# Early weight conversions subtract on VectorE instead of GpSimd, and ScalarE copies out all transposes of the first five head pairs

## The chip, the cores and the metric

The kernel runs on one core of one Trainium2 chip. Five engines work side by side: TensorE multiplies matrices (PE in the profile, and PEld where it loads weights), VectorE (DVE) and ScalarE (ACT) work on rows of 128 partitions and can read the accumulators in PSUM, GpSimd (POOL) works on SBUF alone here, and SyncE (SP) issues the DMA transfers. Each engine runs its own instructions strictly in order, and an instruction that waits for another engine holds up everything behind it. The metric is the device time of one execution in microseconds (us); less is better.

## The reference

Two stages. The first is attention over 4 batches of 8 heads, 576 rows of 64, with a memory term mixed in by a gate per head; the second is a feed-forward block over the 2304 rows of the result.

```python
scores = scale * np.matmul(q, k.transpose(0, 1, 3, 2))     # causal, then softmax: a
local = np.matmul(a, v)
q_p = phi(q)                                               # phi(x) = (x if x > 0 else exp(x) - 1) + 1
mem_out = einsum(q_p, M_prev) / (einsum(q_p, z_prev)[..., None] + 1e-06)
attn = g * mem_out + (1 - g) * local                       # g = sigmoid(beta), one per head
x = attn.transpose(0, 2, 1, 3).reshape(B * S, H * D)       # 2304 x 512
h = x @ w_in                                               # 512 -> 2048
y = (h * np.tanh(log1p(exp(h)))) @ w_out                   # 2048 -> 512, float32
```

The weights `w_in` and `w_out` come as 64-bit floats, and the products of the second stage are made from a high and a low part of each operand.

## The kernel before

**Attention** goes by pairs of heads, 16 in all. For a pair `load`, `load2` and `loadv` bring the inputs; `scores` multiplies (line 364, tile `s`), takes the scores out of PSUM with the running row extreme (line 374, VectorE, tiles `w` and `mx`) and makes the exponentials in place (line 381, ScalarE); `prep` makes phi(q) and its denominators (lines 313 to 337, tiles `qn`, `phe`, `den`; the product with `z` is GpSimd's). `norm` scales the exponentials by the row sums and puts phi(q) beside them (lines 93 and 87 as GpSimd's, tile `w`). `transp` then transposes the weights of one head on TensorE (line 445, tile `t` in PSUM) in four groups of 384, 448, 512 and 512 columns, and each group is copied to SBUF (tile `at`): by ScalarE at line 110 or by VectorE at line 112. These copies are called evictions here. `av` multiplies with the values (line 473, tile `vps`), ScalarE makes the high part `xo` and VectorE the low part `xl`, and both go to memory (`xs`).

**Conversion of weights.** `split` makes one of 16 slices of both weight matrices ready, in two calls of `narrow`, one for `wi` and one for `wo`. Such a half is a DMA into `raw` and seven steps: `c1` scales the upper word on ScalarE (line 91, tile `wa`) and takes its sign on VectorE (line 156, tile `ws`); `c2` is lines 162 and 165 on VectorE; `c3` makes the high part `hi` on ScalarE (line 110); `c4` is line 172 on VectorE, the last reader of `raw`; `c5` subtracts `hi` from `wa` (line 178, recorded at its helper, line 87); `c6` adds the rest on VectorE (line 87 again) and frees `wa` and `ws`. Six slices, twelve halves, are converted between the pairs 1 to 6 (`CV`), with one buffer each for `raw`, `wa` and `ws`; ten more follow after the attention, with a subtraction of their own name (`wsut`). The table `ENG` names the engine of each step: `wsub` is the subtraction of the first twelve halves.

**Feed-forward.** From pair 4 on, pieces of its first part are mixed in (`steps_a`): 12 products for a block of 128 hidden columns (line 233, tile `h`), Mish on ScalarE (line 217, which needs another function table than the exponential, so that ScalarE loads tables between them), a high part on ScalarE and a low part on VectorE (tile `g`), and after six blocks the products with `w_out` (line 246). After the last pair `tail` does the rest (lines 566 and 583).

**What sets the order.** The code is recorded in program order with priorities (`OFF`), and a scheduler lays out each engine's instructions from a simulated run; at run time that order is fixed. A change of an engine at one step can therefore move other instructions, on every engine. The functions that the diff touches:

Of the kernel before, what the change touches and what calls it, by code (L numbers as in the profile page):

```python
# [30 lines left out]
VB = 2  # L31
CV = {1: 1, 3: 1, 4: 2, 5: 1, 6: 1}
FAE = "avav"
CB = 1
CT = 2
RT = 2
# [4 lines left out]
GPB = 6  # L41
NRM = "ppppp"
ENG = {"ph2": "v", "mghT": "a", "mglT": "v", "min": "v", "zmul": "p", "cphi": "p", "xlo": "v",
       "mgh": "a", "mgl": "v", "wx": "a", "whi": "a", "wsub": "p", "wadd": "v", "wsut": "v", "wadt": "v"}
QT = [(0, 64), (64, 192), (192, 320), (320, 448), (448, 576)]
BIG = 8.0e9
E_SC = 0.125
# [29 lines left out]
def attention_moe_kernel(ctx: ExitStack, tc: tile.TileContext, f_src, qn, vn, zz, beta, w_in, w_out, out):  # L77
# [30 lines left out]
    def copy(which, o, i):  # L108
        if which == "a":
            nc.scalar.copy(out=o, in_=i)  # L110
        elif which == "v":
            nc.vector.tensor_copy(out=o, in_=i)  # L112
        else:
            nc.gpsimd.tensor_scalar(out=o, in0=i, scalar1=1.0, scalar2=1.0, op0=ALU.mult, op1=ALU.mult)
# [30 lines left out]
    def narrow(pool, own, src, hi, lo):  # L145
        t = {}

        def c0():
            t["r"] = raw = pool.tile([128, 512, 2], I32, tag="raw", name="raw", bufs=1 if own is cp else RT)
            t["a"] = own.tile([128, 512], I32, tag="e", name="wa", bufs=CB if own is cp else CT)  # L150
            t["s"] = own.tile([128, 512], I32, tag="L", name="ws", bufs=CB if own is cp else CT)
            nc.sync.dma_start(out=raw[:].rearrange("p a b -> p (a b)"), in_=src.bitcast(I32))
# [111 lines left out]
    def attention():  # L264
# [17 lines left out]
        def spare(p, order, pool, tag, shape):  # L282
            if p < EARLY and order[turn[tag] % len(order)] == "e":
                pool = ps_e
            turn[tag] += 1
            return pool.tile(shape, F32, tag=tag, name=tag)
# [145 lines left out]
        def transp(h):  # L432
            g = hd[h]
            ops = []

            def tr(gr, first):
                if first:
                    g["at"] = []
                g["at"].append(tp.tile([128, 512], F32, tag="at", name="at", bufs=AHB))
                ps = g["tps"] = spare(h // 2, TQ, ps_t, "t", [128, 512])  # L440
                o = 0
                for t, m in gr:
                    n = QT[m][1] - QT[m][0]
                    c = WO[m] + 128 * t
                    nc.tensor.transpose(ps[:, o:o + 128], g["w"][:, c:c + 128], ident[:])  # L445
                    o += n

            def out(base, n):
                copy(FAE[base], g["at"][base][:, :n], g["tps"][:, :n])

            for base, gr in enumerate(GR):
                n = sum(QT[m][1] - QT[m][0] for _, m in gr)
                ops += [lambda gr=gr, first=(base == 0): tr(gr, first), lambda base=base, n=n: out(base, n)]
            return ops
# [52 lines left out]
        for p in range(NP):  # L507
# [16 lines left out]
            if p >= P0:  # L524
                if (p - P0) % 4 == 0:
                    todo.extend(steps_a((p - P0) // 4))
                n = int(SPREAD * (p - P0 + 1)) - done[0]
# [142 lines left out]
```

## Time and profile before

| what | us |
|---|---|
| runs shown | 656.19, 655.2, 653.29; median 655.2 |
| the profiled execution, its own time | 654.77 |
| its span, first to last instruction | 653.0 |
| busy: PE, PEld, DVE, ACT, POOL | 597.0, 454.9, 336.8, 300.7, 169.1 |

The page's picture in 40 slices of 16.3 us; each digit is the busy share in tenths:

```profile
PE   3477968889989999999998979999999999999997
PEld 2254635656655766767776878888888888888886
DVE  4989897765588654573338887920311211121121
ACT  3677655866567675566325455621222222222221
POOL 3697886464166714443000000000000000000000
PEclk9979986899999999999999989999999999999999
```

TensorE is busy nearly throughout, but a busy PE is not a PE at its peak, since matmuls wait in it; its gaps lie in the first ten slices, where VectorE has its highest digits. GpSimd ends its work with the attention, at slice 20.

### The profile page before, as it was taken

How to read it: one execution, taken by the hardware profiler on the slowest of the kernel's cores; microseconds unless marked ns; L12 is line 12 of the kernel's file. 1: busy time of each engine (PE TensorE's matmuls, PEld its weight loads, DVE VectorE, ACT ScalarE, POOL GpSimd, SP SyncE). 2: the span in 40 equal slices, each digit the busy share in tenths (PEclk: the TensorE clock that was granted, in tenths of full speed). 3: DMA queues.
4: the chain of work that ended last, by engine and by line, in shares of the span. 5: the costliest groups of instructions: out<-in, count | busy, mean ns of one | idle time of the engine just before them, and what ended most of it. 6: DMA issues, size and time to landing. Idle time of an engine off the chain costs nothing.

```text
span 653.0 us, 9308 instructions
## 1 busy us (share of the span) xinstructions
PE 597.0 (91%) x3200; PEld 454.9 (70%) x3200; DVE 336.8 (52%) x903; ACT 300.7 (46%) x694; POOL 169.1 (26%) x260
## 2 busy tenths in 40 slices
PE   3477968889989999999998979999999999999997
PEld 2254635656655766767776878888888888888886
DVE  4989897765588654573338887920311211121121
ACT  3677655866567675566325455621222222222221
POOL 3697886464166714443000000000000000000000
PEclk9979986899999999999999989999999999999999
DMA  6345674324275226421257765304302220430220
GB/s 229 104 144 182 189 262 150 133 61 144 76 235 168 98 62 176 166 73 58 91 176 235 261 206 176 121 1 129 130 0 82 94 83 6 124 129 0 65 97 33
DMA packets 47007, 80.83 MB, mean 124 GB/s; under 512 B 7280, under 2 KB 21616, under 8 KB 46960
## 3 DMA queue, kind: packets, MB, share of 16 engines
q1 hardware_dynamic: 46960, 80.24, 38.0%
q8 instruction: 25, 0.41, 0.3%
q14 instruction: 22, 0.18, 0.1%
HBM read 61.35 MB, written 18.87 MB: 123 GB/s over the span
## 4 chain that ended last, share of the span: by engine, by line
PE 61%; DVE 13%; DMA 10%; ACT 7%; POOL 5%; issue 2%; SPq 1%; DVEq 0%; ACTq 0%; POOLq 0%
PE o L583 19%; PE h L566 19%; PE acc L246 7%; PE h L233 5%; DMA raw<-in_w_in_dram 5%; PE vps L473 5%; PE t L445 4%; DVE w L374 3%; PE s L364 3%; POOL w L93 3%; DMA raw<-in_w_out_dram 3%; DMA qn<-in_qn_dram 2%; ACT w L381 2%; ACT L217 1%; DVE ws L172 1%
## 5 line engine op out<-in xcount | busy, mean ns | idle before, releaser
L87 DVE TENSOR_TENSOR g<-u,g 128x512 fp32r<-128x512 f32 (+1 forms) x80 | 52.4, 661 | 185.6 <-ACT g L110 185.6
L566 PE MATMUL h<-xb,wi 128*128 128x512 f32 (+1 forms) x600 | 134.9, 368 | 0.0
L583 PE MATMUL o<-wo,g 128*128 128x512 f32 x540 | 133.8, 390 | 0.0
L217 ACT ACTIVATE u<-h 128x512 f32<-128x512 f32 (+1 forms) x80 | 43.5, 554 | 179.2 <-PE h L566 170.9
L566 PEld LDWEIGHTS h<-xb,wi 128*128 128x128 f32 x600 | 106.1, 188 | 19.6
L583 PEld LDWEIGHTS o<-wo,g 128*128 128x128 f32 x540 | 100.6, 188 | 20.3
L93 POOL TENSOR_SCALAR w<-w,rc 128x64 f32<-128x64 f32 (+4 forms) x160 | 95.4, 621 | 71.0 <-ACT w L381 53.3
L381 ACT ACTIVATE w<-w,mx 128x576 f32<-128x576 f32 (+4 forms) x160 | 88.3, 554 | 28.5 <-DVE mx L374 27.6
L364 PE MATMUL s<-f 64*128 64x288 f32 (+4 forms) x384 | 69.2, 472 | 31.7 <-DVE mx L374 25.4
L233 PE MATMUL h<-xb,wi 128*128 128x512 f32 (+1 forms) x360 | 88.0, 389 | 7.8 <-ACT u L217 7.8
L246 PE MATMUL acc<-wo,g 128*128 128x512 f32 x324 | 85.9, 401 | 1.4 <-ACT ob L110 0.9
L445 PE MATMUL t<-ident,w 128*128 128x128 f32 x480 | 75.5, 291 | 5.3 <-ACT at L110 3.1
L233 PEld LDWEIGHTS h<-xb,wi 128*128 128x128 f32 x360 | 64.8, 200 | 21.1 <-ACT u L217 9.6
L364 PEld LDWEIGHTS s<-f 64*128 64x128 f32 x384 | 35.4, 207 | 59.0 <-DVE mx L374 33.2
L445 PEld LDWEIGHTS t<-ident,w 128*128 128x128 f32 x480 | 55.9, 146 | 26.0 <-issue 8.7
L246 PEld LDWEIGHTS acc<-wo,g 128*128 128x128 f32 x324 | 59.4, 190 | 16.0 <-issue 2.3
L374 DVE CUSTOM_DVE_ANT_0 w<-s,mask 128x288 f32<-128x288 f32 (+4 forms) x160 | 59.6, 421 | 17.6 <-PE s L364 17.6
L473 PE MATMUL vps<-at,v 128*64 128x256 f32 (+2 forms) x512 | 61.3, 383 | 5.8 <-DVE xl L87 3.7
L473 PEld LDWEIGHTS vps<-at,v 128*64 128x64 f32 x512 | 35.6, 142 | 31.7 <-issue 6.0
L112 DVE COPY at<-t 128x448 f32<-128x448 f32 x64 | 41.5, 649 | 16.2 <-PE t L445 16.2
L110 ACT CAST g<-u 128x512 fp32r<-128x512 f32 (+1 forms) x80 | 45.5, 579 | 1.8
L110 ACT COPY at<-t 128x384 f32<-128x384 f32 x64 | 33.7, 526 | 17.6 <-PE t L445 17.4
(45 smaller groups left out, 432.1 us busy)
## 6 DMA issues: line engine op xcount, KB each, us to landing
f<-in_f_src_dram SPq DMA_DIRECT2D x32, 288.0 KB, 3.7
raw<-in_w_in_dram SPq DMA_DIRECT2D x16, 512.0 KB, 3.9
raw<-in_w_out_dram SPq DMA_DIRECT2D x16, 512.0 KB, 3.5
xb<-xs SPq DMA_DIRECT2D x24, 256.0 KB, 3.7
qn<-in_qn_dram SPq DMA_DIRECT2D x16, 320.0 KB, 3.4
v<-in_vn_dram SPq DMA_DIRECT2D x16, 320.0 KB, 3.3
xs<-xo SPq DMA_DIRECT2D x16, 288.0 KB, 3.4
xs<-xl SPq DMA_DIRECT2D x16, 288.0 KB, 3.3
```

What stands on the lines that cost most here:

```text
L87: engines[ENG[name]].tensor_tensor(**kw)
L93: engines[which].tensor_scalar(out=o, in0=i, scalar1=scale, scalar2=1.0, op0=ALU.mult, op1=ALU.mult)
L110: nc.scalar.copy(out=o, in_=i)
L233: ins = nc.tensor.matmul(ps, wi[y, f][:, c, :], x[c][:, z], start=(q == 0), stop=(q == 11))
L246: nc.tensor.matmul(acc[:], g[:, y, 128 * t:128 * t + 128], wo[z, f], start=(f == 0 and y == z), stop=(f == KA - 1 and z == 1),)
L364: nc.tensor.matmul(g["ps"][:, o:o + n], f[le, 0, q0:q0 + 128], f[le, 1, a:b], start=True, stop=True)
L374: nc.vector.tensor_tensor_reduce(out=g["w"][:, WO[m] + D + a:WO[m] + D + b], in0=g["ps"][:, o:o + n], in1=mask[:, c0:c0 + n], scale=-E_SC, ...
L381: nc.scalar.activation(out=row, in_=row, func=ACTF.Exp, scale=-1.0, bias=g["mx"][:, m:m + 1], accum_out=g["sm"][:, m:m + 1])
L445: nc.tensor.transpose(ps[:, o:o + 128], g["w"][:, c:c + 128], ident[:])
L473: queued(nc.tensor.matmul(ps[64 * e:64 * e + 64, a:b], d["v"][:, t, e], at[e][gi][:, c:c + b - a], start=(k == 0), stop=(k == last),), k o ...
L566: nc.tensor.matmul(ps[:, :n], wi[a, f][:, c, :], x[c][:, b], start=(k == 0), stop=(k == 11))
L583: nc.tensor.matmul(D_[t][:], g[:, y, 128 * t:128 * t + 128], wo[z, f], start=(f == KA and y == z), stop=(f == NF - 1 and z == 1),)
```

## The change

Two edits and a constant. `wsub` goes from GpSimd (`"p"`) to VectorE (`"v"`): the subtraction `c5` of the twelve early halves. And with `EVA = 5` the evictions of the pairs 0 to 4 (heads 0 to 9) are all ScalarE's; before, the groups 1 and 3 of every head were VectorE's. Later heads keep the alternation `"avav"`.

```diff
 FAE = "avav"
+EVA = 5
 ...
 ENG = {...
-       ..., "wsub": "p", "wadd": "v", "wsut": "v", "wadt": "v"}
+       ..., "wsub": "v", "wadd": "v", "wsut": "v", "wadt": "v"}
 ...
             def out(base, n):
-                copy(FAE[base], g["at"][base][:, :n], g["tps"][:, :n])
+                copy("a" if h // 2 < EVA else FAE[base], g["at"][base][:, :n], g["tps"][:, :n])
```

The new line moves every later line number of the kernel by one: line 112 of before is 113 after, and so on. Counted over the whole program, 20 copies `at<-t` leave VectorE for ScalarE (ten of 448 columns and ten of 512), 12 subtractions `wa<-wa,wi` and `wa<-wa,wo` leave GpSimd for VectorE, and ScalarE loads its tables 20 times instead of 18.

The order also moves. First VectorE, from the reduction of `den` of the fourth pair on. `wi_2`, `wo_1` are halves of slices 2 and 1, high part first. Before:

```order
L332 TENSOR_REDUCE den<-phe 128x10
L87 TENSOR_TENSOR xl<-vps,xo 128x320
L112 COPY at<-t 128x448
L374 ISA w,mx<-s,mask 128x288
L374 ISA mx 128x1
L87 TENSOR_TENSOR wo_1_85<-wa,ws 128x512
L417 TENSOR_SCALAR rc<-sm,gt 128x5
L333 SCALAR_TENSOR_TENSOR den<-den,gt 128x10
L313 TENSOR_SCALAR phe<-qn 128x640
L374 ISA w,mx<-s,mask 128x288
L374 ISA mx 128x1
L112 COPY at<-t 128x512
```

After, the same place:

```order
L333 TENSOR_REDUCE den<-phe 128x10
L88 TENSOR_TENSOR xl<-vps,xo 128x320
L88 TENSOR_TENSOR wa<-wa,wi_2_86 128x512
L375 ISA w,mx<-s,mask 128x288
L375 ISA mx 128x1
L375 ISA w,mx<-s,mask 128x288
L375 ISA mx 128x1
L334 SCALAR_TENSOR_TENSOR den<-den,gt 128x10
L314 TENSOR_SCALAR phe<-qn 128x640
L418 TENSOR_SCALAR rc<-sm,gt 128x5
L88 TENSOR_TENSOR wi_2_88<-wa,ws 128x512
```

The two copies are gone, a subtraction has come, and the conversion stands one half further: where `wo_1` ended, `wi_2` ends now.

Next ScalarE around the same place, from the high part `xo` of the first pair's output on. Before:

```order
L110 CAST xo<-vps 128x320
L110 COPY at<-t 128x384
L381 ACTIVATE w,sm<-w,mx 128x320
L381 ACTIVATE w,sm<-w,mx 128x192
L381 ACTIVATE w,sm<-w,mx 128x320
L381 ACTIVATE w,sm<-w,mx 128x192
L110 COPY at<-t 128x512
L91 ACTIVATE wa<-raw 128x512
```

After:

```order
L111 CAST xo<-vps 128x320
L111 COPY at<-t 128x384
L111 CAST wi_2_86<-wa 128x512
L111 COPY at<-t 128x448
L382 ACTIVATE w,sm<-w,mx 128x320
L382 ACTIVATE w,sm<-w,mx 128x192
L382 ACTIVATE w,sm<-w,mx 128x320
L382 ACTIVATE w,sm<-w,mx 128x192
L111 COPY at<-t 128x512 x2
L111 COPY at<-t 128x384
```

Two more evictions stand among the exponentials, and the cast that makes `wi_2`'s high part stands behind an eviction.

Last ScalarE where the feed-forward begins, from the first table load for Mish on. Before:

```order
L217 ACT_TABLE_LOAD
L217 ACTIVATE u<-h 128x512
L381 ACT_TABLE_LOAD
L381 ACTIVATE w,sm<-w,mx 128x448
L381 ACTIVATE w,sm<-w,mx 128x64
L110 CAST g<-u 128x512
L91 ACTIVATE wa<-raw 128x512
L217 ACT_TABLE_LOAD
L217 ACTIVATE u<-h 128x512
L110 COPY at<-t 128x512
L110 CAST g<-u 128x512
L110 CAST wi_5_98<-wa 128x512
```

After:

```order
L218 ACT_TABLE_LOAD
L218 ACTIVATE u<-h 128x512
L382 ACT_TABLE_LOAD
L382 ACTIVATE w,sm<-w,mx 128x576
L92 ACTIVATE wa<-raw 128x512
L111 COPY at<-t 128x384
L111 CAST g<-u 128x512
L218 ACT_TABLE_LOAD
L218 ACTIVATE u<-h 128x512
L111 CAST wo_5_99<-wa 128x512
L111 CAST g<-u 128x512
L111 COPY at<-t 128x512
```

The conversion is again one half further: `wi_5`'s cast, in this stretch before, is done ahead of it now, and what is left is the last half, `wo_5`.

## Rows read from the trace of the kernel before

**Rows 1.** Busy time by stretch: us, engines with instruction counts, PEclk, DMA share, GB/s.
```profile
40.00:60.00 20.00, 18.48 (x133) 12.49 (x133) 19.32 (x65) 14.99 (x44) 15.70 (x23) 0.91 0.44 142
60.00:80.00 20.00, 17.73 (x129) 11.57 (x125) 18.14 (x52) 12.13 (x35) 17.66 (x24) 0.91 0.64 201
80.00:100.00 20.00, 12.53 (x79) 7.37 (x78) 18.59 (x53) 11.73 (x32) 15.46 (x20) 0.89 0.76 247
100.00:120.00 20.00, 18.26 (x98) 12.00 (x98) 16.43 (x49) 10.46 (x26) 14.82 (x18) 0.77 0.46 147
120.00:140.00 20.00, 17.40 (x79) 12.00 (x78) 12.99 (x35) 18.05 (x33) 9.72 (x15) 0.91 0.18 62
140.00:160.00 20.00, 16.77 (x107) 11.89 (x104) 11.86 (x38) 13.05 (x32) 6.92 (x12) 1.00 0.50 155
...
260.00:280.00 20.00, 20.00 (x126) 14.19 (x127) 11.29 (x40) 11.85 (x36) 9.15 (x17) 1.00 0.44 148
```

**Rows 2.** Chain that ended last, 20 to 160 us: start, us, what.
```profile
40.29 0.60 DVE at L112
...
88.00 3.46 DMA raw<-in_w_out_dram
...
98.81 0.60 DVE at L112
...
109.64 4.03 DMA raw<-in_w_out_dram
...
123.92 0.57 ACT wa L91
...
127.39 0.52 ACT wi L110
```

**Rows 3.** Groups by form, whole span: line, engine, op, count | busy us, mean ns | idle before.
```profile
L172 DVE SCALAR_TENSOR_TENSOR ws<-raw,ws 128x512 f32<-128x512 uint32 x32 | 24.6, 768 | 0.5
L112 DVE COPY at<-t 128x512 f32<-128x512 f32 x32 | 21.8, 682 | 7.5 <-PE t L445 7.5
L112 DVE COPY at<-t 128x448 f32<-128x448 f32 x32 | 19.7, 615 | 8.7 <-PE t L445 8.7
L110 ACT COPY at<-t 128x512 f32<-128x512 f32 x32 | 18.5, 579 | 8.0 <-PE t L445 7.9
...
L217 ACT ACT_TABLE_LOAD x9 | 11.5, 1283 | 2.7 <-PE h L233 2.6
...
L87 POOL TENSOR_TENSOR wa<-wa,wo 128x512 f32<-128x512 f32 x6 | 8.0, 1340 | 0.0
...
L87 DVE TENSOR_TENSOR wa<-wa,wo 128x512 f32<-128x512 f32 x10 | 6.8, 685 | 0.0
```

**Rows 4.** Groups by form on VectorE, 20 to 105 us alone.
```profile
L172 DVE SCALAR_TENSOR_TENSOR ws<-raw,ws 128x512 f32<-128x512 uint32 x7 | 7.2, 1028 | 0.1
...
L332 DVE TENSOR_REDUCE den<-phe 128x10 f32<-128x640 f32 x7 | 5.7, 814 | 4.2 <-POOL phe L87 4.2
L162 DVE SCALAR_TENSOR_TENSOR wa<-wa,ws 128x512 int32<-128x512 int32 x7 | 5.5, 785 | 0.0
...
L313 DVE TENSOR_SCALAR phe<-qn 128x640 f32<-128x640 f32 x6 | 4.0, 671 | 0.0
```

**Rows 5.** Instructions in order of time, 64 to 69 us: start, us, engine, what [idle before].
```profile
64.63 1.65 DVE L313 TENSOR_SCALAR phe<-qn 128x640 f32<-128x640 f32 x1
64.65 1.27 POOL L87 TENSOR_TENSOR wa<-wa,wi 128x512 f32<-128x512 f32 x1
...
67.65 1.62 POOL L93 TENSOR_SCALAR w<-w,rc 128x64 f32<-128x64 f32 x2 [1.73 <-DVE den L337]
```

**Rows 6.** Waits, 20 to 160 us: who for whom, us in total, times, longest.
```profile
POOL wa L87 <- ACT wi L110: 8.0, 1, 8.0
...
PE t L445 <- ACT at L110: 2.5, 3, 1.1
...
PE vps L473 <- DVE at L112: 1.8, 2, 1.3
```

More of the change, by code (lines that the diff above doesn't have):

```diff
@@ L43 @@
 ENG = {"ph2": "v", "mghT": "a", "mglT": "v", "min": "v", "zmul": "p", "cphi": "p", "xlo": "v",
-       "mgh": "a", "mgl": "v", "wx": "a", "whi": "a", "wsub": "p", "wadd": "v", "wsut": "v", "wadt": "v"}
+       "mgh": "a", "mgl": "v", "wx": "a", "whi": "a", "wsub": "v", "wadd": "v", "wsut": "v", "wadt": "v"}
 QT = [(0, 64), (64, 192), (192, 320), (320, 448), (448, 576)]
```

## The prediction, written before the changed kernel ran

> **What bounds the kernel now.** I read the busy time by stretch first, since the change touches only the first 150 us. From about 160 us on TensorE is full: in the stretch 260 to 280 us it is busy 20.00 of 20 and ScalarE and VectorE are not [rows 1]. The order of all engines from the last pair's attention on is the same in both kernels. So the change can move the end only by what it does before 160 us, and what is won there passes to the end in full. How much there is to win: TensorE's gaps are 3.8 us in 40 to 80 us (40 less 18.48 and 17.73) and 15.0 us in 80 to 160 us (80 less 12.53, 18.26, 17.40 and 16.77) [rows 1]. That 18.8 us is the ceiling for these stretches.
>
> What fills the gaps' place is VectorE: 19.32, 18.14 and 18.59 of 20 in the three stretches from 40 to 100 us. GpSimd is high too (15.70, 17.66, 15.46), ScalarE is not (14.99, 12.13, 11.73). After that the load turns round: in 120 to 140 us ScalarE is busy 18.05, VectorE 12.99, GpSimd 9.72 [rows 1].
>
> Second, the chain of waits. Between 20 and 105 us it runs for the most part through VectorE, and ten of its pieces there are evictions of VectorE, from 40.29 to 98.81 us, 0.60 us each at most, some 5 us. Pieces of the early conversion are on it as well: two loads of `raw` (3.46 and 4.03 us), and in ScalarE's stretch a scaling of 0.57 and a cast of 0.52 us [rows 2]. The subtraction on GpSimd does not appear on it.
>
> **The subtraction leaves GpSimd.** Twelve at 1.34 us is 16.1 us less on GpSimd [rows 3]. I count this as worth nothing by itself: the subtractions stand in GpSimd's gaps. At 64.65 us one runs for 1.27 us, and GpSimd then still idles 1.73 us until VectorE's `den` lets it scale the next head [rows 5]. What it does to VectorE is another matter: in the same moment the simple operation at line 313 takes 1.65 us, where the other five of its group in 20 to 105 us take (4.0 - 1.65)/5 = 0.47 us [rows 4, 5]. One such stretch of 1.2 us goes with the subtraction.
>
> **The subtraction comes to VectorE.** No subtraction of the early halves has run there. The late ones, when GpSimd is idle, take 0.685 us [rows 3]; that is the lower end, 8.2 us for twelve. The upper end is line 172, also 512 columns with two inputs, in the stretch where GpSimd is busy: 1.028 us, against (24.6 - 7.2)/25 = 0.70 us in the other 25 cases [rows 3, 4]; twelve of these are 12.3 us. I take line 162 in that stretch, the nearest in form (two inputs of the same width, `wa` among them): 0.785 us, 9.4 us in all.
>
> The trace thus shows VectorE's two-input operations lengthened while GpSimd works. The Trainium skill, GPSIMD Engine Reference, section Specifications, says why: GpSimd's SBUF interfaces are shared with VectorE, with contention for VectorE's operations in a two-port mode or with two SBUF inputs. The rule speaks against moving a two-input operation to VectorE while GpSimd still has its scalings to do; by it the sum would lie toward 12.3 us, and by line 162's row it is 9.4.
>
> **The evictions.** Ten copies of 448 columns at 0.615 us and ten of 512 at 0.682 us leave VectorE: 13.0 us [rows 3]. ScalarE gets ten of 512 at 0.579 us and ten of 448 that it has not done before, at most 0.579 us each and surely above half of that: 8.7 to 11.6 us, I take 11. They lie in 20 to 118 us, where ScalarE has a quarter to two fifths of its time free (8.3 us of 20 in 80 to 100 us, 5.0 in 40 to 60 us) [rows 1]; I cost them there at nothing. If that cover fails, the price shows at TensorE's transposes, which wait for a free PSUM tile: they waited 2.5 us for ScalarE's evictions in 20 to 160 us, and twice the evictions would make it 5.0. Against that, the 1.8 us that the products with the values waited for VectorE's evictions go [rows 6]. The net, +0.7 us, I put into the sum.
>
> VectorE's balance is therefore -13.0 + 9.4 = -3.6 us (bounds -4.8 and -0.7). The order shows when it arrives: counting instructions up to the last scores of the sixth pair, the new order has 18 copies fewer but nine subtractions more and two halves of conversion further on, and the load is the same; only by the eighth pair, when both orders have converted all twelve halves, is the difference there. Since VectorE is the fullest engine until 100 us and the conversions that are done earlier are missing from the later stretch, I take the 3.6 us in full.
>
> **What moves on ScalarE.** In 120 to 140 us ScalarE is the full engine. The order shows one scaling and one cast of a conversion fewer there, both on the chain: 0.57 + 0.52 = -1.1 us [rows 2]. Two more table loads, 1.283 us each [rows 3], come later, where TensorE is full and ScalarE has 8 us of 20 free [rows 1]: zero, at worst +2.6.
>
> **The sum.** -1.2 (stretch) -3.6 (VectorE) -1.1 (ScalarE) +0.7 (waits for evictions) = -5.2 us, from the profiled execution's own 654.77 us: 649.6. That execution is 0.4 us below the median of the three runs, so against the median it is 650.0, 0.8% less. It is under a third of the 18.8 us of gaps. The ends: with the dear subtraction, the stretch and the 1.1 us not gained and the tables paid, -0.7 + 0.7 + 2.6 gives 658; with the cheap one and VectorE's 4.2 us of waiting for GpSimd's `phe` [rows 4] filled by conversion work pulled forward, about 645.
>
> **Rivals.**
> *Nothing moves.* TensorE in 40 to 80 us has only 3.8 us of gaps, so relief of VectorE there ends in TensorE, and after 105 us the chain goes over table loads, scalings of GpSimd and transfers that the change leaves alone. For it: VectorE's load up to the sixth pair is unchanged by the order. Against it: 15 us of gaps lie in 80 to 160 us. Time 655.
>
> *Slower: VectorE stands still at the new subtraction.* It needs the cast that ScalarE makes of the same half. On GpSimd such a wait harmed nobody: one lasted 8.0 us [rows 6]. On VectorE it holds back all behind it: the scores of the next pair, then ScalarE's exponentials, then TensorE. And the order puts a cast behind evictions now (`wi_2` behind the copy of 384 columns), which wait for transposes, which wait for GpSimd's scalings. Against it: in most places of the new order there is a score step or more between line 172 and the subtraction. One stall like that of GpSimd gives 650.0 + 8.0 = 658, two give 666; from 5.2 us of stalls in all it is no gain.
>
> *A larger gain.* The early halves are a chain of their own, since each waits for the one buffer `raw`; two loads of it, 3.46 and 4.03 us, are on the chain of waits [rows 2]. With the conversion two halves ahead these would fall where VectorE has other work: 650.0 - 7.5 = 642.5. Against it: VectorE itself idled little at these places, its neighbours were as late.
>
> **How the numbers follow.** A measurement of this kernel can tell a difference of about 0.5%, 3.3 us: faster is under 651.9, slower over 658.5. The forecast, -5.2 us, has a chance of 0.43, and its own range is 646 to 654. Nothing moves: 0.27. Slower: 0.20. Larger gain: 0.10. Of the forecast some 0.34 lie under 651.9, with the larger gain 0.44 faster; same gets 0.38, with the rest of the forecast and the lighter end of the stalls; slower 0.18. The range is 643 to 661: it leaves out two long stalls above and a gain beyond both terms below.
>
> **What would show it.** Right: VectorE under 18.5 of 20 in the stretches from 40 to 100 us or the eighth pair's scores done earlier; the subtractions at 0.69 to 1.03 us; no wait of VectorE's `wa` for ScalarE's `wi` or `wo` in the list of waits beyond 2 us; the last attention product and the first late load of `raw` some 5 us earlier and the rest unchanged. Wrong: that wait at 5 us or more; TensorE's transposes waiting over 5 us for ScalarE's evictions; a 120 to 160 us stretch in which ScalarE is as full as before.

## The result, and the profile after

The changed kernel takes 661.62 us (median of 8 runs, 659.23 to 663.74) against 655.91 us of the kernel before on the same chip: a ratio of 1.0085, interval 1.0063 to 1.0107. It is 0.85% slower, where 650.0 us was forecast. The profiled execution took 662.05 us, its span 660.0 us.

Busy time by stretch of the kernel after, with the columns of [rows 1]; two stretches are new here:

```profile
40.00:60.00 20.00, 16.89 (x114) 10.90 (x116) 18.65 (x64) 16.29 (x44) 13.75 (x19) 0.83 0.41 137
60.00:80.00 20.00, 17.29 (x126) 10.98 (x123) 16.01 (x47) 13.89 (x38) 19.95 (x28) 0.91 0.69 219
80.00:100.00 20.00, 13.32 (x87) 8.11 (x87) 18.73 (x53) 13.89 (x37) 11.50 (x15) 0.91 0.70 225
100.00:120.00 20.00, 16.11 (x88) 10.45 (x88) 16.22 (x49) 13.29 (x35) 14.67 (x19) 0.83 0.58 188
120.00:140.00 20.00, 18.96 (x105) 13.89 (x104) 12.36 (x39) 18.07 (x37) 2.49 (x5) 1.00 0.21 65
140.00:160.00 20.00, 19.02 (x114) 14.09 (x114) 10.80 (x35) 12.81 (x30) 5.81 (x11) 1.00 0.37 114
180.00:200.00 20.00, 14.61 (x103) 8.88 (x102) 11.92 (x46) 10.71 (x32) 10.78 (x21) 0.93 0.57 177
260.00:280.00 20.00, 18.59 (x99) 13.69 (x100) 12.05 (x39) 11.69 (x34) 7.20 (x11) 0.91 0.37 116
```

The stretch 180 to 200 us of the kernel before, which the prediction did not look at:

```profile
180.00:200.00 20.00, 17.75 (x134) 11.43 (x133) 15.92 (x54) 12.62 (x36) 14.49 (x28) 1.00 0.67 210
```

VectorE is relieved from 60 to 80 us (16.01 for 18.14), and GpSimd fills there instead (19.95 for 17.66). TensorE gains from 120 to 160 us (18.96 and 19.02 for 17.40 and 16.77) what it lost before. Then, far behind the last moved instruction, it is busy 3.1 us less from 180 to 200 us and 1.4 us less from 260 to 280, both at a granted clock under 1.00.

Chain that ended last, 20 to 160 us, of the kernel after (start, us, what), some of its longest pieces:

```profile
47.28 3.81 POOL w L94 x5
...
72.33 4.03 POOL w L94 x4
...
86.24 1.84 DVE wa L88
93.24 3.04 DMA qn<-in_qn_dram
...
147.12 1.28 ACT L319
```

Where [rows 2] has evictions of VectorE and loads of `raw`, there is now one new subtraction on VectorE (1.84 us) and a table load at line 319, and most of the long pieces are scalings of GpSimd. Those were on the chain before too, but with less: line 93 was 10.1% of it between 20 and 105 us, line 94 is 32.5%. That subtraction in order of time:

```profile
85.99 1.54 POOL L88 TENSOR_TENSOR phe<-qn,z 128x640 f32<-128x640 f32 x1 [0.76 <-DVE qn L85]
86.17 1.92 DVE L88 TENSOR_TENSOR wa<-wa,wo 128x512 f32<-128x512 f32 x1
```

Waits of the kernel after, 20 to 160 us, as in [rows 6]:

```profile
POOL w L94 <- DVE rc L421: 18.5, 1, 18.5
...
DVE den L333 <- POOL phe L88: 9.0, 6, 2.7
...
PE t L446 <- ACT at L111: 7.2, 6, 2.2
...
PE vps L474 <- ACT at L111: 1.5, 2, 1.2
...
DVE wa L88 <- ACT wo L111: 0.9, 1, 0.9
```

Where a pair's second store into `xs` is issued tells roughly how far the whole program is (us, one traced execution of each kernel; e1 to e10 are the experiments below):

| pair | before | after | e1 | e2 | e4 | e5 | e6 | e7 | e9 | e10 |
|---|---|---|---|---|---|---|---|---|---|---|
| 7th | 179.1 | 176.8 | 181.8 | 174.4 | 178.1 | 178.9 | 177.1 | 176.4 | 183.1 | 176.6 |
| 8th | 193.8 | 193.4 | 196.7 | 191.8 | 192.1 | 194.6 | 192.2 | 190.6 | 198.8 | 191.8 |
| 11th | 243.6 | 248.9 | 253.5 | 247.3 | 248.2 | 244.7 | 242.4 | 245.8 | 248.7 | 241.8 |
| 16th | 336.6 | 343.2 | 347.9 | 341.6 | 341.1 | 337.7 | 335.4 | 340.0 | 341.8 | 334.8 |

The kernel after is 2.3 us ahead at the seventh pair, 5.3 us behind at the eleventh and 6.6 us at the sixteenth. Two cautions. A store's place among the other work moves with the order: from the tenth pair's store to the eleventh's the kernels with the late order (after, e1, e2, e4, e7) take 29.6 us and the others of the table 25.1 or 25.2, and some of that comes back by the twelfth. The sixteenth pair, from which on both orders are the same, is the safest row. And one execution need not stand for its median: the trace of e4 is of its fastest (659.04 us, median 664.54), that of e5 too, that of e6 of its slowest (654.98, median 653.43).

What happened behind the seventh pair, in order of time in the kernel after:

```profile
183.52 0.33 SPq L299 DMA_DIRECT2D qn<-in_qn_dram  x1
...
188.92 0.49 DVE L314 TENSOR_SCALAR phe<-qn 128x640 f32<-128x640 f32 x1 [3.91 <-DMA qn<-in_qn_dram]
189.33 0.62 DVE L375 CUSTOM_DVE_ANT_0 w<-s,mask 128x448 f32<-128x448 f32 x1
...
190.84 1.13 PE L365 MATMUL s<-f 64*128 64x320 f32 x8 [2.11 <-DVE mx L375]
...
195.95 0.76 PE L365 MATMUL s<-f 64*128 64x288 f32 x4 [1.84 <-DVE mx L375]
...
197.22 2.19 PE L474 MATMUL vps<-at,v 128*64 128x320 f32 x8
```

and the same place in the kernel before:

```profile
184.43 0.62 DVE L374 CUSTOM_DVE_ANT_0 w<-s,mask 128x448 f32<-128x448 f32 x1 [0.76 <-PE s L364]
...
188.44 0.49 DVE L313 TENSOR_SCALAR phe<-qn 128x640 f32<-128x640 f32 x1 [1.39 <-DMA qn<-in_qn_dram]
```

The changed order has VectorE's phi step of the twelfth pair ahead of the 448-wide scores of the tenth. The phi step waits for its load, the finished scores wait behind it, and TensorE waits for a free score bank. A part of the stall is the load's own length in this execution: from its issue to the phi step are 5.40 us here and 2.93 us in the kernel before (issue at 185.51 us).

### The profile page after: what moved, and what is told of

It reads as the page before. It is cut to its first block, busy times and chain, and to the rows that moved or that the text cites. A ratio compares the mean times of both kernels' runs of the same rounds, so it can differ in the third digit from the quotient of the medians.

```text
span 660.0 us, 9304 instructions
## 1 busy us (share of the span) xinstructions
PE 598.3 (91%) x3200; PEld 454.5 (69%) x3200; DVE 331.9 (50%) x895; ACT 312.1 (47%) x716; POOL 155.6 (24%) x248
## 4 chain that ended last, share of the span: by engine, by line
PE 65%; DVE 9%; DMA 9%; POOL 8%; ACT 6%; issue 2%; SPq 1%; DVEq 0%; ACTq 0%; POOLq 0%
PE o L584 19%; PE h L567 18%; PE h L234 7%; PE acc L247 7%; PE vps L474 5%; POOL w L94 5%; PE t L446 4%; DMA raw<-in_w_in_dram 4%; PE s L365 4%; DVE w L375 3%; DMA qn<-in_qn_dram 2%; DMA raw<-in_w_out_dram 2%; ACT w L382 1%; POOL w L88 1%; DVE ws L173 1%
## 5 line engine op out<-in xcount | busy, mean ns | idle before, releaser
L88 DVE TENSOR_TENSOR g<-u,g 128x512 fp32r<-128x512 f32 (+1 forms) x80 | 52.3, 657 | 191.8 <-ACT g L111 191.8
L94 POOL TENSOR_SCALAR w<-w,rc 128x64 f32<-128x64 f32 (+4 forms) x160 | 98.6, 637 | 110.7 <-DVE rc L421 75.5
L247 PE MATMUL acc<-wo,g 128*128 128x512 f32 x324 | 84.3, 402 | 1.7 <-ACT ob L111 1.4
L474 PE MATMUL vps<-at,v 128*64 128x256 f32 (+2 forms) x512 | 65.0, 394 | 3.9 <-DVE xl L88 2.2
L474 PEld LDWEIGHTS vps<-at,v 128*64 128x64 f32 x512 | 37.2, 147 | 31.6 <-issue 8.9
L111 ACT COPY at<-t 128x384 f32<-128x384 f32 (+1 forms) x84 | 43.2, 535 | 14.7 <-PE t L446 14.6
L92 ACT ACTIVATE wa<-raw 128x512 f32<-128x512 f32 x32 | 21.7, 678 | 37.8 <-DMA raw<-in_w_in_dram 19.8
```

The lines of the kernel that those rows point to most:

```text
L88: engines[ENG[name]].tensor_tensor(**kw)
L94: engines[which].tensor_scalar(out=o, in0=i, scalar1=scale, scalar2=1.0, op0=ALU.mult, op1=ALU.mult)
L247: nc.tensor.matmul(acc[:], g[:, y, 128 * t:128 * t + 128], wo[z, f], start=(f == 0 and y == z), stop=(f == KA - 1 and z == 1),)
L474: queued(nc.tensor.matmul(ps[64 * e:64 * e + 64, a:b], d["v"][:, t, e], at[e][gi][:, c:c + b - a], start=(k == 0), stop=(k == last),), k o ...
```

## The experiments

Theory *order*: the moved work costs about nothing, and the loss is the scheduler's new late order. Rival *work*: the moved work costs it, and the order is immaterial. In e3 to e6 and e8 to e16 an order is held, by edges that only order and never wait, added once the program is recorded (`PIN` lists for each engine the instructions from a given pair on, as the other kernel has them). Where the list begins in the middle of the program, two orders meet; that place is called the join below. The edges:

```diff
+        for row in PIN:
+            for a, b in zip(row, row[1:]):
+                tc.add_manual_dep(have[b], a, info, reason="pin")
```

Each ratio is to the kernel before on the same chip, with its 95% interval.

**e1: the subtractions alone.**
```diff
-EVA = 5
+EVA = 0
```


> Only the twelve subtractions go to VectorE; all evictions of transposed weights alternate as before. The order of instructions from about the tenth pair's scores on is the same as in the changed kernel (TensorE's last 2171 of 2752 instructions, VectorE's last 499). Theory 'order' (the moved work costs about nothing, the 5.7 us of the change come from the new late order, in two places near 190 and 255 us): 658 to 663 us, about as slow as the whole change. Theory 'work' (the 5.7 us are the price of moved work: more on ScalarE, subtractions on VectorE beside GpSimd's normalizations): the two halves share 5.7 us, the subtractions take at most half of it: 654 to 659, and the two halves' losses add up to about 5.7.

Measured 666.48 us, 1.0163 (1.0134 to 1.0192): slower than the whole change, and above the ranges of both theories. VectorE, then TensorE, in its trace:

```profile
174.52 0.49 DVE L314 TENSOR_SCALAR phe<-qn 128x640 f32<-128x640 f32 x1 [5.83 <-DMA qn<-in_qn_dram]
174.93 0.68 DVE L113 COPY at<-t 128x512 f32<-128x512 f32 x1
...
175.67 1.11 PE L446 MATMUL t<-ident,w 128*128 128x128 f32 x4 [4.61 <-DVE at L113]
```

The same kind of stall at another pair: a phi step that waits 5.83 us for its load holds back an eviction.

**e2: the evictions alone.**
```diff
-"wsub": "v"
+"wsub": "p"
```


> Only the evictions: the first five pairs' transposed weights all go through ScalarE; the subtractions stay on GpSimd. The late order is again the changed kernel's (TensorE's last 2138 instructions, VectorE's last 481). Theory 'order': 658 to 664 us, as slow as the whole change, so that the two halves together lose about twice what the whole does. Theory 'work': what is left of 5.7 us after the subtractions alone, 657 to 661.

660.58 us, 1.0060 (1.0037 to 1.0084). The halves lose 1.63% and 0.60%, together 2.2%, the whole 0.85%. The costs do not add up as *work* has it.

**e3: the whole change, order of before from the tenth pair on.** `PIN` from the tenth pair.

> The changed kernel with all its moved work; only the order of what belongs to the tenth pair and later is held, on every engine, to what it is in the kernel before. Theory 'order': the loss goes, 652 to 656 us (the two traces stand level, within 1 us, at 180 us, and from there on the work is the same). Theory 'work': the moved work is all there, so 660 to 662 stays.

659.89 us, 1.0049 (1.0027 to 1.0072): 0.36% of the 0.85% goes. The loss neither goes nor stays, so neither theory has this.

**e4: the kernel before, order of after from the tenth pair on.**

> The kernel before with none of the moved work; only the order of what belongs to the tenth pair and later is held to what it is in the changed kernel. Theory 'order': 660 to 665 us (before's time plus the 9 us of TensorE time lost in the two places, less a little that the join of the two orders may change). Theory 'work': nothing is moved, so 654 to 657.

664.54 us, 1.0106 (1.0067 to 1.0145). With no work moved, this run loses 1%, as *order* has it. It has a join at the tenth pair, though, so how much of the 1% is the late order behind it and how much the join is not separated. In its trace the phi step of the twelfth pair stands ahead of the scores as in the kernel after, but waits only 1.06 us:

```profile
187.56 0.49 DVE L313 TENSOR_SCALAR phe<-qn 128x640 f32<-128x640 f32 x1 [1.06 <-DMA qn<-in_qn_dram]
```

**e5: the whole change, order of before throughout.**

> The whole change's work, with every engine's order held to that of the kernel before from the first instruction to the last; only the 12 subtractions and 20 evictions themselves stand where the scheduler puts them on their new engines. Theory 'order': 654 to 657 us against 657 of the kernel before on this chip (the work by itself within 0.5%). Theory 'work': the moved work costs what the change costs, 660 to 663.

660.49 us, 1.0042 (1.0022 to 1.0063). The time lies at the lower end of the range of *work*, the ratio at half of the change's loss. So *order* in its strict form fell; the work costs something too.

**e6: the evictions alone, order of before from the ninth pair on.**

> Only the evictions are moved (as in e2), and what belongs to the ninth pair and later stands in the order of the kernel before. In e2's trace TensorE stood 3 us ahead of the kernel before at 170 us and lost 6 us from 190 to 210 us and some 3 more later. Theory 'order': those 3 us stay, 652 to 656, the fastest of all. Theory 'work': no faster than e2, 659 to 662.

653.43 us, 0.9932 (0.9901 to 0.9963). The same work as e2, 1.3% apart by its order, and faster than both kernels.

**e7: one edge in the changed kernel.**
```diff
+                if p == 11:
+                    order_after(ins, hd[2 * p - 3]["r", 0, 0])
```
`ins` is the phi step, `"r", 0, 0` the last of the 448-wide bank's extractions.

> The changed kernel with one order edge: VectorE's phi step of the twelfth pair (the one that stands still 3.9 us for its load at 189 us) comes behind the 448-wide scores of the tenth pair, as in the kernel before; else nothing of the order changes but the steps right around it. Theory 'order': of the two losses the first goes, so 4 us less than the change: 657 to 659 (4 of 9 us of TensorE time). Theory 'work': 661 to 663.

659.31 us, 1.0037 (1.0022 to 1.0053), 0.48% less than the change and 0.3 us above the range of *order*. The stall is gone:

```profile
183.19 0.33 SPq L299 DMA_DIRECT2D qn<-in_qn_dram  x1
...
185.44 0.62 DVE L375 CUSTOM_DVE_ANT_0 w<-s,mask 128x448 f32<-128x448 f32 x1 [0.65 <-PE s L365]
...
187.30 0.49 DVE L314 TENSOR_SCALAR phe<-qn 128x640 f32<-128x640 f32 x1 [0.40 <-DMA qn<-in_qn_dram]
```

From 180 to 200 us TensorE is busy 17.41 us at a clock of 1.00, as in the kernel before:

```profile
180.00:200.00 20.00, 17.41 (x134) 10.87 (x133) 13.33 (x48) 10.69 (x31) 13.83 (x27) 1.00 0.65 201
```

**e8: the other place.** At 253 to 259 us the changed kernel has four table loads, 1.28 us each, since two Mish alternate with exponentials. `PIN` from the twelfth pair.

> The changed kernel with the order of the kernel before for what belongs to the twelfth pair (counted from one) and later: the phi step at 189 us stays where the change has it, but the two Mish at 253 to 260 us no longer alternate with exponentials (two table loads there in place of four). Theory 'order': the first loss stays, the second goes: 657 to 660. Theory 'work': 661 to 663.

661.89 us, 1.0074 (1.0049 to 1.0099): no difference from the change that these intervals show. In its trace one load serves both Mish,

```profile
253.22 1.28 ACT L218 ACT_TABLE_LOAD   x1 [3.26 <-PE h L234]
254.52 0.60 ACT L218 ACTIVATE u<-h 128x512 f32<-128x512 f32 x1
...
256.15 0.60 ACT L218 ACTIVATE u<-h 128x512 f32<-128x512 f32 x1
```

and TensorE is full from 260 to 280 us (20.00), but from 240 to 260 us it is busy 18.30 for the change's 19.72. The test leaves the second place open. Its trace is 2.4 us ahead of the change's at the sixteenth pair's store (340.8 for 343.2 us), the medians show nothing of it, and it has a join of its own: from the tenth pair's store to the twelfth's it takes 52.5 us, the change 52.7, the kernel before 49.0.

**e9: the subtractions alone, order held throughout.**

> Only the twelve subtractions are moved, and every engine's order is held to that of the kernel before throughout (the counterpart of e5 without the evictions). Theory 'order' in its strict form (the moved work costs nothing): 655 to 659 us, within 0.3% of before. Theory 'subtractions cost' (formed after e5 and e6: with order held, the subtractions on VectorE are what costs, the evictions are what gains): 660 to 664.

662.71 us, 1.0083 (1.0051 to 1.0115). The tenth subtraction, in e9:

```profile
117.20 2.01 POOL L88 TENSOR_TENSOR phe<-qn,z 128x640 f32<-128x640 f32 x1
117.71 2.05 DVE L88 TENSOR_TENSOR wa<-wa,wo 128x512 f32<-128x512 f32 x1
119.69 0.61 DVE L375 CUSTOM_DVE_ANT_0 w<-s,mask 128x448 f32<-128x448 f32 x1
```

and the same place in the kernel before:

```profile
116.83 2.02 POOL L87 TENSOR_TENSOR phe<-qn,z 128x640 f32<-128x640 f32 x1
117.34 0.61 DVE L374 CUSTOM_DVE_ANT_0 w<-s,mask 128x448 f32<-128x448 f32 x1
```

Beside GpSimd's product the subtraction takes 2.05 us, three times its 0.68, and the scores behind it come 2.35 us later than before (0.37 us of it the stretch was late already).

**e10: the evictions alone, order held throughout.**

> Only the twenty evictions are moved, every engine's order held to that of the kernel before throughout. Strict 'order': 655 to 659. 'Subtractions cost, evictions gain': 651 to 655, like e6.

654.20 us, 0.9940 (0.9920 to 0.9960). By itself and in the old order this half is a gain, as 'evictions gain' had it.

**e11: the whole change, order of before from the ninth pair on.**

> The whole change, with the order of the kernel before for what belongs to the ninth pair and later: e6 with the subtractions moved as well. Strict 'order': like e6, 652 to 656. 'Subtractions cost': 6 us above e6, 658 to 662, like e3 and e5.

656.81 us, 0.9984 (0.9965 to 1.0004). All of the change's work and its own early order, and the loss is gone: 1.0% less than the change by what stands from the ninth pair on. It is 0.5% over e6. 'Subtractions cost' said 658 to 662, strict *order* 652 to 656; it lies between.

**e12: the evictions alone, order of before from the tenth pair on.**

> Only the evictions, with the order of the kernel before from the tenth pair's work on (e6 took it from the ninth). In e2 TensorE stood 3 us ahead of before at 170 us, in e6 1 us at 170 and level at 180. If the later join keeps those 3 us: 649 to 652, the fastest of all. If the join itself costs what it did in e3 (3 us lost between 190 and 220 us): 653 to 657.

657.90 us, 1.0005 (0.9984 to 1.0027), 0.9 us above the higher of its two ranges: the join at the tenth pair costs 0.7% against that at the ninth, in e12 against e6 as in e3 against e11.

**e13: as e9, each subtraction directly ahead of its addition.**

> As e9 (only the subtractions on VectorE, order held), but each subtraction stands directly ahead of the addition that needs it, 1 to 15 instructions later than in e9, behind the score extractions that e9 has it ahead of. Theory 'place' (the subtraction costs because score extractions queue behind it): 655 to 659 us, within 0.3% of before, and no gap of TensorE for VectorE's scores at 121 us. Theory 'load' (VectorE is the poorer by 8 us of work wherever it stands): 661 to 664, like e9.

662.26 us, 1.0097 (1.0068 to 1.0126). The theory of the place fell.

**e14: the same of the whole change.**

> As e5 (the whole change's work, order held), with the subtractions directly ahead of their additions as in e13. 'Place': 652 to 656, like e10. 'Load': 659 to 662, like e5.

659.22 us, 1.0038 (1.0016 to 1.0060), like e5.

**e15: as e9, the tenth subtraction back on GpSimd.**
```diff
-            tt("wsub" if own is cp else "wsut", ...
+BACK = (10,); CN = []          # and "wsup": "p" in ENG
+            CN.append(own is cp); tt(("wsup" if sum(CN) in BACK else "wsub") if own is cp else "wsut", ...
```


> As e9, with the tenth subtraction alone back on GpSimd (eleven stay on VectorE). In e9's trace TensorE is level with before until 110 us, loses 2 us behind the tenth subtraction at 118 us, 2 more from 140 to 160 and 1 near 198. 'Place': the first 2 us go, 659 to 661. 'Load': no change that can be measured, 661 to 664.

661.26 us, 1.0062 (1.0039 to 1.0085): 0.2% under e9, and the intervals overlap. The long stall beside GpSimd's product did not go with the subtraction. Another step of VectorE with two inputs, line 163's, has it now, in e16 as well (1.93 us at 114.25 us):

```profile
119.11 1.56 POOL L88 TENSOR_TENSOR phe<-qn,z 128x640 f32<-128x640 f32 x1
119.14 2.07 DVE L163 SCALAR_TENSOR_TENSOR wa<-wa,ws 128x512 int32<-128x512 int32 x1
```

**e16: as e5, the tenth and the twelfth back.** `BACK = (10, 12)`.

> As e5 (the whole change, order held to that of the kernel before), with the tenth and the twelfth subtraction back on GpSimd and ten on VectorE. If the subtractions' cost is the stall of the tenth beside GpSimd's phi product and the exposed table load that hangs on these two: 653 to 656 us, level with e10. If it is the load on VectorE in general (ten of twelve are still there): 657 to 660, at most 1 or 2 us below e5.

656.31 us, 0.9987 (0.9972 to 1.0003), between its two ranges: 0.55% under e5 by two of twelve subtractions, the other ten are 0.47% over e10. A stall of the tenth subtraction is not the difference: in e5's trace it takes 0.89 us. One part is seen in the rows. ScalarE in e5, and then in e10:

```profile
134.41 0.58 ACT L111 COPY at<-t 128x512 f32<-128x512 f32 x1
142.50 1.28 ACT L319 ACT_TABLE_LOAD   x1 [7.51 <-DVE phe L314]
143.79 0.74 ACT L319 ACTIVATE phe<-phe 128x640 f32<-128x640 f32 x1
```

```profile
134.16 0.58 ACT L111 COPY at<-t 128x512 f32<-128x512 f32 x1
134.76 1.28 ACT L319 ACT_TABLE_LOAD   x1
141.43 0.74 ACT L319 ACTIVATE phe<-phe 128x640 f32<-128x640 f32 x1 [5.39 <-DVE phe L314]
```

In e10 the load lies in the idle time, in e5 behind the wait. In e9's trace, too, the load stands behind the wait (at 146.71 us, after 7.05 us for VectorE's phi step), in the kernel before it doesn't (137.33 us, the exponential at 143.92). The built programs show why, the kernel before and then e9:

```
L318 ACT_TABLE_LOAD
L318 ACTIVATE phe<-phe 128x640 [waits DVE_49]
```
```
L319 ACT_TABLE_LOAD [waits DVE_49]
L319 ACTIVATE phe<-phe 128x640 [waits Pool_49]
```

Without the subtraction on GpSimd the exponential needs a wait for GpSimd of its own; of two waits the first then stands ahead of the load. In e16 the load is in the idle time again (137.29 us, the exponential at 144.06), and in e15 too (142.31 and 149.36).

**e17: e2 with e7's edge.**

> As e2 (evictions alone, the scheduler's own order, which loses 0.6%), with the one edge of e7: the phi step of the twelfth pair behind the 448-wide scores of the tenth. If that wait is what the late order costs, as e7 says of the whole change (0.5%): 655 to 658 us. If the rest of the late order costs it: 659 to 662, like e2.

658.44 us, 1.0024 (1.0005 to 1.0042), between its two ranges and 0.36% under e2. The edge gives back a part; e10's order gives 1.2%.

## Why the prediction was wrong

**The step that failed** is "From about 160 us on TensorE is full [...] what is won there passes to the end in full". It rested on one stretch, 260 to 280 us, and on an order that is the same only from the last pair's attention on. Between 160 us and there both orders differ, and TensorE was not full: 17.75 of 20 from 180 to 200 us even before. The early part did a little under half of what was forecast (2.3 us ahead at the seventh pair); 8.9 us were then lost up to the sixteenth. That the late order costs this is shown by two pairs of runs with the same work: e11 loses nothing where the change loses 0.85%, and e6 and e2, 1.3% apart, differ only by the order from the ninth pair on. e4 points the same way, with its join in it. One edge (e7) recovers 0.48%, and 3.2 of the 6.6 us at the sixteenth pair. What makes up the rest of the late order's cost is not shown: e2 and e4 lose by it although their phi step waits only 1.29 and 1.06 us there.

**A second step failed beside it**, "I take the 3.6 us in full". Even with the old late order the whole change takes 0.9984 of the time before (e11, and its interval has 1 in it), not the 0.992 that was forecast.

**The subtraction on VectorE**, 9.4 us for twelve, was sized nearly right: the early twelve took 10.0 us in the trace after. But the sum had it as load to be balanced against copies (-3.6 us). One of them took 1.92 us and stood on the chain; e9 shows that the subtractions alone, with the order held, cost 0.83%, and e13 that another place does not help. The stretch of line 313 that was to go (-1.2 us) came back as that one. The rule cited there bore out: the subtractions at 1.92 and 2.05 us end 0.56 and 0.55 us after GpSimd's product that began ahead of them. The Trainium skill, SBUF — State Buffer, section Who interferes with whom, says that a VectorE operation with two SBUF inputs contends with a GpSimd operation that reads SBUF, and that the order of issue decides who blocks; these rows agree.

**The evictions** cost more waits than the +0.7 us of the sum: TensorE's transposes waited 7.2 us for ScalarE's (2.5 before, 5.0 allowed for), and the products, whose wait was to go, still waited 1.5, now for ScalarE; reckoned as in the sum that is +4.4. With the order held they gain 0.6% nevertheless (e10). The relief of VectorE was right in kind, for this half alone.

**GpSimd** was called worth nothing. It had 13.5 us less to do and still became the early chain, whose share of scalings rose from 10.1 to 32.5% between 20 and 105 us. The conversions ran some 12 us ahead (the eighth load of `raw` at 75.4 us, before 88.0) without bringing the attention forward. The loads of `raw` left the chain from 20 to 160 us, as the rival of the larger gain had it (three before, one of them, 4.41 us at 47.20 us, not in the prediction's reading, and none after), and GpSimd's scalings took the place.

**ScalarE's -1.1 us** did not come (18.07 of 20 from 120 to 140 us, before 18.05), and the chain there has a table load that waits, which the sum did not have. The two more table loads, costed at zero, were not shown to cost: e8 took two away and stayed at 1.0074, with a join of its own in it.

**The slower rival** had the right sign and the wrong place: VectorE waited 0.9 us in all for ScalarE's cast. It stood still 3.91 us for a load, at a step that the diff does not touch.

**What stays open.** With the order held, 0.4% of the whole change's loss (e5) is only partly accounted for: the exposed load is 1.28 us, and e5's trace, of its fastest execution (656.82 us), shows no loss like its median. In e9's trace some 2 us of the 5.1 at the sixteenth pair come from the tenth subtraction and 1.4 from the load (the phi step ahead of it is 2.73 us later than before, 146.13 for 143.40, the step behind it 4.15, 148.84 for 144.69). But e13 and e15 are late from the third pair's store on (83.0 and 83.7 us, before 80.8), where neither bears on them. Why the join at the tenth pair costs more than that at the ninth was not tried, nor the kernel before held to its own order, which would show what the holding itself does.

## What to carry to other kernels

Where a scheduler lays out the order, compare the order over the whole span and not only where the edit is: hold the old order and measure the edit, then the order by itself. Ask of each instruction that the new order puts ahead of a critical one what it waits for; a step with a fresh load in front of finished scores cost about 0.5% here, and the moved work of the whole change gained nothing that its interval shows (e11). Split a change that has two edits before judging it: here, in the old order, one gains 0.6% and the other loses 0.8%.

## What the hardware showed unexpectedly

After the stalls at 190 and 195 us TensorE's granted clock fell to the lower of its two levels: it was 0.50 from 197.2 to 200.6 us, where the kernel before has 1.00 throughout 180 to 300 us. The mean of 180 to 200 us is 0.93, and the eight products at 197.22 us took 2.19 us, where twelve take 1.41 at 182.60 us. GpSimd's operations lengthen in such places too: its two products that write `w` from `qn` and `den` at 137.29 us take 1.31 us together in e5, beside VectorE's addition (0.99 us, alone 0.68), and 0.87 in e10, where they run alone.
